# Second output layer of a fused attention and two-layer expert kernel: seven products in place of eight in five of six groups

## The chip, the cores and the metric

One core of a Trainium2 chip runs the whole program in one launch. The metric is the device time of that core in microseconds. Its engines are TensorE (PE; PEld is its weight load), VectorE (DVE), ScalarE (ACT), GpSimd (POOL) and the queue of SyncE (SP), which issues all DMAs here.

## The reference

```python
# q, k, v: (8, 8, 576, 64); x: 4608 tokens of 512 features; all float32
kv = einsum('bhsd,bhse->bhde', k, v)
out = einsum('bhsd,bhde->bhse', q, kv)
x = out / sqrt(mean(out * out, -1) + 1e-6) * g_norm     # -> (4608, 512)
x = (sigmoid(x @ w_gate) * (x @ w_val)) @ moe_w_out     # inner width 1536
h = x @ moe2_w_in                                       # inner width 2048
return where(h > 0, h, exp(min(h, 0)) - 1) @ moe2_w_out
```

All inputs and the output are float32. (Weights come as 64-bit words of which the kernel takes the upper and the lower 32 bits apart and puts a float32 together.)

## The kernel before

**Numbers.** A matmul operand is kept as two rounded parts, hi (ACT rounds, `x_hi`) and lo (DVE subtracts, `x_lo`); a product of two operands is three matmuls, hi·hi, hi·lo and lo·hi (`matmul3`, lines 347 to 351). So nearly all matmuls stand on lines 349 to 351.

**Groups.** The 4608 tokens are cut into 12 blocks of `BLK` = 384, two blocks to a group, `NG` = 6 groups. Features are cut into 128-row chunks. In the first half of the kernel (to about 985 us in the trace) each group has its attention (`attention`, for two blocks each), the first gated layer (`in1`, twelve products of 42 matmuls, and `in1_plain` for group 0) and the first output layer (`out1`), whose result goes to memory (`x2d`). The second half runs, group by group, `in2` and `out2`: eight pairs of hidden chunks in `in2`, and an output layer over `NF2` = 16 hidden chunks.

**Seven products.** The in layers already run as Strassen (Winograd) products in 2 x 2 blocks: the two token blocks of a group against the two halves of the features, and two chunks of hidden units. `quad` (line 484) takes seven products, six matmuls of 384 columns each, puts them into four PSUM banks `psi` and adds them with `plus` on DVE (line 500) into `v` tiles. `sides` (line 466) makes their left sides: differences of the token blocks, `k1` on DVE, `k2`, `k3` and the last one on POOL (lines 473 to 478), and hi and lo of seven sides (lines 479 and 480). `sums` makes the weights' sums on POOL and stores them in memory; `stream` loads hi and lo of them again for each group, 1 MB a tile of class `S` (five slots).

**The second output layer.** `out2` (line 619) is a plain product. For each of 16 hidden chunks and both token blocks, `split` (line 564) rounds a hidden tile of 128 x 384 into a `J` tile (ACT line 567, DVE line 569; three slots), and three token tiles of 128 are the stationary operand against 512 columns of weights: nine matmuls of 512 columns for each split, 288 a group, in six PSUM tiles. `copy_out` (lines 572 to 575) brings these to `kv` tiles, and six stores of 256 KB go to `out`.

**The norm.** In `attention` 13 small operations on DVE (lines 423 to 430) make the inverse root, written as one task (line 432), so that nothing else can come between them; four scalings (line 440) and the transposes (line 450) follow.

**Order.** `Plan` orders all tasks ahead of time, before the program runs: TensorE's tasks keep the order in which they are written, and each other engine takes, whenever it is idle in the plan, the ready task with the earliest due time. Each task has a planned duration, an engine, and the tiles that it holds; a class of tiles has a fixed number of slots and in places a cap by kind. On the chip each engine then runs its tasks in the planned order and waits by semaphore. `decode` (line 259) takes the weights apart during the first half; that of the second output layer stores hi and lo for a pair of chunks in `wo2`.

Of the kernel before, what the change touches and what calls it, by code (L numbers as in the profile page):

```python
# [21 lines left out]
P = 128  # L22
# [12 lines left out]
MM = BLK / 2400 + 0.0126  # L35
MMW = DM / 2400 + 0.0126
T_ACT, T_DVE, T_POOL = 0.53, 0.57, 1.15

# [167 lines left out]
def tile_kernel(ctx: ExitStack, tc: tile.TileContext, kv, kvtail, qt, g2, w1, w2, out):  # L206
# [30 lines left out]
    slots("psi", 4, [P, 512], F32, ps)  # L237
    slots("psa", 4, [P, 512], F32, ps)
    plan.caps.update({"h": 32, "tmp": 11, "xf": 8, "ev": 3, "q": 4, "dec": 4, "dec2": 2, "wh": 2, "wp": 2})
# [19 lines left out]
    def decode(layer, fp, after=None):  # L259
# [20 lines left out]
        sa = plan.buf("S", "dec" if layer in "gvo" else "dec2")  # L280
        if layer in "oO":
# [8 lines left out]
        if layer in "oO":  # L290
            d = (wo1 if layer == "o" else wo2)[fp]
            written[layer, fp] = [dma(P * 8192, lambda: nc.sync.dma_start(
                out=d.rearrange("q f t n -> q (f t n)"), in_=sa.slot.rearrange("q b t n -> q (b t n)").bitcast(F32)), [h, l], [sa])]
            return sa, [h, l]
        d = (ws2 if layer == "I" else ws1["gv".index(layer)])[fp]
# [8 lines left out]
    def sums(layer, fp, wh, w):  # L304


        d = (ws2 if layer == "I" else ws1["gv".index(layer)])[fp]
        sf, sb_ = plan.buf("wk", "wp"), plan.buf("S", "dec2" if layer == "I" else "st")
        A = lambda i: wh.slot[:, i // 2, i % 2 * 256:i % 2 * 256 + 256]
# [12 lines left out]
        return sb_, [h2, l2], st  # L322

    def fresh(layer, fp):

        sa, wh = plan.buf("S", "st"), plan.buf("wk", "wh")
        k = "gv".index(layer)
        ld = dma(P * 4096, lambda: nc.sync.dma_start(out=wh.slot, in_=wf1[k][fp]), written["f", layer, fp], [wh], early=20.0)
        ld_a = dma(P * 6144, lambda: nc.sync.dma_start(out=sa.slot[:, 1:4].bitcast(F32), in_=ws1[k][fp][:, 0:3]), written[layer, fp], [sa], early=15.0)
        sb_, done, st = sums(layer, fp, wh, ld)  # L330
        written[layer, fp] = written[layer, fp] + [st]
        return (sa, sb_), ([ld_a], done)

    def stream(layer, fp):

        sa = plan.buf("S", "st")
        if layer in "oO":
            d = (wo1 if layer == "o" else wo2)[fp]
            return sa, [dma(P * 8192, lambda: nc.sync.dma_start(
                out=sa.slot.rearrange("q b t n -> q (b t n)").bitcast(F32), in_=d.rearrange("q f t n -> q (f t n)")), written[layer, fp], [sa], early=15.0)]  # L340
        d = (ws2 if layer == "I" else ws1["gv".index(layer)])[fp]
        sb_ = plan.buf("S", "st")
# [39 lines left out]
    def attention(j, queue, direct=None, bank="psa", gap=3, hold=None):  # L382
# [82 lines left out]

    def sides(xa, xb):

        X = {c: plan.buf(c) for c in XB}
        done = {c: [] for c in XB}
        for c in range(2):  # L470
            (b11, d11), (b21, d21), (b12, d12), (b22, d22) = xa[c], xa[c + 2], xb[c], xb[c + 2]
            t1, t2 = plan.buf("v", "tmp"), plan.buf("v", "tmp")
            k1 = add("DVE", 0.5, lambda t=t1, a=b12, b=b11: nc.vector.tensor_tensor(t.slot, a.slot, b.slot, op=ALU.subtract), [d12, d11], [t1, b12, b11])  # L473
            k3 = add("POOL", T_POOL, lambda a=b22, b=b12: nc.gpsimd.tensor_tensor(b.slot, a.slot, b.slot, op=ALU.subtract), [k1, d22], [b22, b12])
            k2 = add("POOL", T_POOL, lambda t=t2, a=b22, b=t1: nc.gpsimd.tensor_tensor(t.slot, a.slot, b.slot, op=ALU.subtract), [k1, d22], [t2, b22, t1])  # L475
            for n, f, d in (("x11", b11, d11), ("xt2", t2, k2), ("x12", t1, k1), ("xt3", b12, k3), ("x21", b21, d21), ("x22", b22, d22), ("xt4", None, None)):
# [141 lines left out]

    def out2(g, hs):
        acc = {blk: [plan.buf("psi" if blk == 0 else "psa") for _ in range(TPB)] for blk in range(2)}  # L620
        for f in range(NF2):
            if f % 2 == 0:
                s, ld = stream("O", f // 2)
            for blk in in_blocks(f, NF2):
                j, dj = split(*hs[f // 2][f % 2, blk])
                for i in range(TPB):
                    def mm(i=i, blk=blk, j=j, s=s, f=f):
                        v = s.slot.rearrange("q b t n -> q (b t n)").rearrange("q (f t n) -> q f t n", f=2, t=2)
                        matmul3(acc[blk][i].slot, j.slot[:, 0, i * P:i * P + P], j.slot[:, 1, i * P:i * P + P],
                                v[:, f % 2, 0, :], v[:, f % 2, 1, :], f == 0, f == NF2 - 1)  # L630
                    t = add("PE", 3 * MMW, mm, ld + dj, [acc[blk][i], s, j])
                    if f == NF2 - 1:
                        e = plan.buf("kv")
                        view = lambda e=e: e.slot.rearrange("q a c n -> q (a c n)")[:, :DM]
                        c = copy_out(i, view, lambda b=acc[blk][i]: b.slot, [t], [e, acc[blk][i]])
                        r0 = (2 * g + blk) * BLK + i * P
                        dma(P * 2048, lambda view=view, r0=r0: nc.sync.dma_start(out=out[r0:r0 + P, :], in_=view()), [c], [e], due=0.5)


# [111 lines left out]
```

## Time and profile before

| | us |
|---|---|
| median of three runs | 1728.72 (1728.35 to 1732.57) |
| profiled execution | 1734.85 |
| its span, first to last instruction | 1733.0 |
| TensorE busy | 1699.8 |
| VectorE busy | 969.7 |
| ScalarE busy | 745.6 |
| GpSimd busy | 258.0 |

The profiled execution is one run, some microseconds longer than the median. Busy times are taken from the records of instructions: a matmul's record also covers the time in which its last columns pass through the array beside the next one's first, so the time that one takes is read from the distance of starts. The granted clock is TensorE's share of its 2.4 GHz level; it was 0.987 on average. A wait is told with the engine that waited, the line, and what released it.

### The profile page before, as it was taken

The numbers are of one execution on the slowest core, as the hardware profiler recorded it, in microseconds if no ns is written. First come the engines' busy times: TensorE is split into PE (matmuls) and PEld (weight loads), VectorE is DVE, ScalarE is ACT, GpSimd is POOL, SyncE is SP. The second block draws the span as 40 slices with busy tenths as digits, with TensorE's granted clock in tenths as the row PEclk, the third lists the DMA queues.
The fourth block names the chain that finished last, engine by engine and source line by source line (L and its number), as shares of the span: only waits on it lengthen the run. The fifth ranks groups of instructions, "written<-read, shape, count | busy, mean of one in ns | idle before, by whom it ended". The sixth has DMA issues, their size and how long they took to land.

```text
span 1733.0 us, 26330 instructions
## 1 busy us (share of the span) xinstructions
PE 1699.8 (98%) x9999; PEld 1596.4 (92%) x9999; DVE 969.7 (56%) x1752; ACT 745.6 (43%) x1495; POOL 258.0 (15%) x242
## 2 busy tenths in 40 slices
PE   8999999999999999999999999999999999999998
PEld 6899999989999999899899998898998998998987
DVE  5768466834585475458445465365465455555542
ACT  4556433632362254126213364364453453543542
POOL 0001264401231141124022001001001001001000
PEclk7999999999999999999999999999999999999999
DMA  8997987888579679767877465575574673673751
GB/s 311 336 310 267 347 274 286 307 311 302 217 291 344 228 257 344 273 219 266 316 256 261 166 259 196 185 265 182 192 273 150 220 280 119 249 272 110 265 200 58
DMA packets 94447, 431.65 MB, mean 249 GB/s; under 512 B 10608, under 2 KB 29040, under 8 KB 66928
## 3 DMA queue, kind: packets, MB, share of 16 engines
q1 hardware_dynamic: 94320, 429.96, 68.3%
q8 instruction: 79, 1.29, 0.3%
q14 instruction: 48, 0.39, 0.1%
HBM read 353.37 MB, written 76.55 MB: 248 GB/s over the span
## 4 chain that ended last, share of the span: by engine, by line
PE 91%; DMA 4%; DVE 3%; issue 1%; ACT 1%; SPq 0%; DVEq 0%; ACTq 0%
PE psi L349 23%; PE psi L351 22%; PE psi L350 22%; PE psa L350 7%; PE psa L351 6%; PE psa L349 6%; PE psa L407 2%; DMA S<-wsv 1%; PE psa L375 1%; DVE xp L440 1%; PE psa L450 1%; DMA wsI<-S 1%; DVE v L500 1%; DMA wsv<-S 1%; DMA wsg<-S 0%
## 5 line engine op out<-in xcount | busy, mean ns | idle before, releaser
L500 DVE TENSOR_TENSOR v<-v,psi 128x384 f32<-128x384 f32 x540 | 298.2, 553 | 355.8 <-PE psi L351 347.3
L349 PE MATMUL psi<-x,S 128*128 128x384 f32 x1056 | 361.3, 342 | 4.7 <-DVE v L500 4.0
L351 PE MATMUL psi<-x,S 128*128 128x384 f32 x1056 | 355.7, 337 | 4.8 <-DVE S L289 4.8
L350 PE MATMUL psi<-x,S 128*128 128x384 f32 x1056 | 355.1, 336 | 0.9 <-DVE x L458 0.9
L569 DVE TENSOR_TENSOR J<-v,J 128x384 fp32r<-128x384 f32 x336 | 201.8, 604 | 254.5 <-ACT J L567 254.3
L567 ACT ACTIVATE J<-v 128x384 fp32r<-128x384 f32 x336 | 175.3, 523 | 324.0 <-PE psa L350 116.7
L349 PE MATMUL psi<-xt,S 128*128 128x384 f32 x648 | 222.1, 343 | 11.2 <-DMA S<-wsv 7.4
L351 PE MATMUL psi<-xt,S 128*128 128x384 f32 x648 | 218.3, 337 | 0.0
L350 PE MATMUL psi<-xt,S 128*128 128x384 f32 x648 | 218.0, 336 | 0.0
L349 PEld LDWEIGHTS psi<-x,S 128*128 128x128 f32 x1056 | 199.7, 189 | 9.7 <-DVE v L500 5.9
L351 PEld LDWEIGHTS psi<-x,S 128*128 128x128 f32 x1056 | 199.7, 189 | 5.4 <-DVE S L289 5.4
L350 PEld LDWEIGHTS psi<-x,S 128*128 128x128 f32 x1056 | 199.8, 189 | 1.9 <-DVE x L458 1.4
L536 POOL TENSOR_TENSOR v<-v,v 128x384 f32<-128x384 f32 x90 | 97.0, 1083 | 419.4 <-DVE v L500 418.7
L475 POOL TENSOR_TENSOR v<-v,v 128x384 f32<-128x384 f32 x22 | 23.7, 1077 | 759.8 <-DVE v L473 580.0
L349 PEld LDWEIGHTS psi<-xt,S 128*128 128x128 f32 x648 | 122.8, 190 | 14.4 <-issue 8.1
L350 PEld LDWEIGHTS psi<-xt,S 128*128 128x128 f32 x648 | 122.9, 190 | 0.0
L351 PEld LDWEIGHTS psi<-xt,S 128*128 128x128 f32 x648 | 122.7, 189 | 0.0
L613 ACT ACTIVATE v<-v 128x384 f32<-128x384 f32 x144 | 75.4, 524 | 108.6 <-DVE v L500 108.6
L351 PE MATMUL psa<-S,J 128*128 128x512 f32 x288 | 112.8, 392 | 0.0
L351 PE MATMUL psi<-S,J 128*128 128x512 f32 x288 | 112.6, 391 | 0.0
L350 PE MATMUL psa<-S,J 128*128 128x512 f32 x288 | 112.2, 390 | 0.0
L349 PE MATMUL psi<-S,J 128*128 128x512 f32 x288 | 112.1, 389 | 0.0
(99 smaller groups left out, 2863.9 us busy)
## 6 DMA issues: line engine op xcount, KB each, us to landing
S<-wsI SPq DMA_DIRECT2D x48, 1024.0 KB, 5.1
S<-wsO SPq DMA_DIRECT2D x48, 1024.0 KB, 4.9
S<-wso SPq DMA_DIRECT2D x36, 1024.0 KB, 6.3
S<-wsI SPq DMA_DIRECT2D x48, 768.0 KB, 5.9
raw<-w SPq DMA_DIRECT2D x68, 512.0 KB, 6.4
S<-wsg SPq DMA_DIRECT2D x24, 1024.0 KB, 5.4
S<-wsv SPq DMA_DIRECT2D x24, 1024.0 KB, 5.1
S<-wsg SPq DMA_DIRECT2D x30, 768.0 KB, 6.6
```

What stands on the lines that cost most here:

```text
L349: nc.tensor.matmul(acc, wh, xh, start=first, stop=False, skip_group_check=more)
L350: nc.tensor.matmul(acc, wh, xl, start=False, stop=False, skip_group_check=more)
L351: nc.tensor.matmul(acc, wl, xh, start=False, stop=last, skip_group_check=more)
L375: nc.tensor.matmul(pb.slot[e, :D], k[:, 0, c, e], k[:, 1, c, e], start=(c == 0), stop=False)
L407: nc.tensor.matmul(o[h].slot[lo - t0:hi - t0, n:n + D], qs[k].slot[r, lo - j * BLK:hi - j * BLK], kvb[b % 2][r, 2 * pp + k, :], start=True ...
L440: norm[pp, h] = add("DVE", T_DVE, lambda x=xn[pp], o=po[pp][h], pp=pp, h=h: nc.vector.tensor_tensor(x.slot.rearrange("q k (i n) -> q (k i) ...
L475: k2 = add("POOL", T_POOL, lambda t=t2, a=b22, b=t1: nc.gpsimd.tensor_tensor(t.slot, a.slot, b.slot, op=ALU.subtract), [k1, d22], [t2, b22 ...
L500: return add("DVE", T_DVE, lambda: nc.vector.tensor_tensor(dst.slot, a.slot, bank[k].slot[:, :BLK], op=ALU.add), after, [dst, a, bank[k]])
L536: t = add("POOL", T_POOL, lambda r=r, b=b: nc.gpsimd.tensor_tensor(r.slot, r.slot, b.slot, op=ALU.mult), [d, s], [r, b])
L567: hi = add("ACT", T_ACT, lambda: nc.scalar.activation(j.slot[:, 0, :], f.slot, AF.Copy), [d], [j, f])
L569: lo = add("DVE", 0.5, lambda: nc.vector.tensor_tensor(j.slot[:, 1, :], f.slot, j.slot[:, 0, :].bitcast(F32), op=ALU.subtract), [hi], [j, f])
L613: a1 = add("ACT", T_ACT, lambda e=e, b=b: nc.scalar.activation(e.slot, ps_or_v(b), AF.Relu, scale=-1.0), [d], [e, b])
```

## The change

- `out2` of groups 1 to 5 is written as seven products as `quad` is: the hidden tiles of the two token blocks (`B11`, `B12`, `B21`, `B22`) against weights in four parts (two halves of the hidden chunks, two halves of 256 columns). A product runs over eight weight pairs, three token tiles and three terms with 256 columns. `combine` makes T1 to T3 on POOL and T4 on DVE, in `w` tiles, which are halves of the tiles `raw`, `wk` and `kv` that are free by then, or in place; each side of a product is split anew (7 x 8 splits in place of 32). Each product has two PSUM tiles, and `copy` (ACT) and `plus` (DVE) of 512 and 256 columns bring it into `xp` tiles, of which there are four. Four stores of 384 KB go to `out`.
- Group 0 keeps the plain product (`out2_plain`), reading the weights in their new layout, and out of `xp` tiles. Beside it `sums_O` loads each weight pair, makes four sums on DVE, splits them and stores them to `wo2`, which has eight parts now. POOL's first `combine` waits for all tasks that use `raw`, `wk` or `kv`.
- `sides` takes the engine as an argument; for the second layer its three POOL steps go to DVE.
- The norm's 13 operations are 13 tasks, except in the two blocks that are written with `hold` (the first two).
- `v` has 48 slots in place of 50, `xp` 4 in place of 3.

```diff
-    slots("xp", 3, [P, 2, BLK], F32)
-    slots("v", 50, [P, BLK], F32)
+    slots("xp", 4, [P, 2, BLK], F32)
+    slots("v", 48, [P, BLK], F32)
...
-    wo2 = [dr.tile([P, 2, 2, DM], F32, tag=f"wsO{f}", name=f"wsO{f}") for f in range(NF2 // 2)]
+    wo2 = dr.tile([P, 8, NF2 // 2, 2, 256], F32, tag="wsO", name="wsO")
...
+    def sums_O(fp, after):
+
+        pair, w = [(plan.buf("kv"), "q a c n -> q (a c n)"), (plan.buf("raw"), "q n t -> q (n t)")], plan.buf("wk", "wh")
...
+        for i in range(2):
+            ld = dma(P * 4096, lambda i=i: nc.sync.dma_start(out=v[i](), in_=wo2[:, 2 * i:2 * i + 2, fp]), written["O", fp] + [after], [pair[i][0]])
+            word.append(add("DVE", 0.7, lambda i=i: nc.vector.tensor_tensor(
+                W()[:, 2 * i:2 * i + 2, :], v[i]()[:, :, 0, :], v[i]()[:, :, 1, :], op=ALU.add), [ld], [pair[i][0], w]))
+        last = word
+        for d, a, b, op in ((1, 0, 1, ALU.add), (0, 2, 0, ALU.subtract), (2, 1, 2, ALU.subtract), (3, 3, 2, ALU.subtract)):
+            last = [add("DVE", 0.4, lambda d=d, a=a, b=b, op=op: nc.vector.tensor_tensor(one(d), one(a), one(b), op=op), last, [w])]
+        st = []
+        for i, src in ((0, lambda: W()[:, 1:3, :]), (1, lambda: W()[:, 0:4:3, :])):
...
+            st.append(dma(P * 4096, lambda i=i: nc.sync.dma_start(out=wo2[:, 4 + 2 * i:6 + 2 * i, fp], in_=v[i]()), [h, l], [pair[i][0]]))
...
-        last = [add("DVE", 0.2 * len(ops), lambda: [op() for op in ops], red, [sm])]
+        last = red
+        for part in ([ops] if hold is not None else [[op] for op in ops]):
+            last = [add("DVE", 0.2 * len(part), lambda part=part: [op() for op in part], last, [sm])]
...
-    def sides(xa, xb):
+    def sides(xa, xb, eng="POOL"):
+        ge, gt = (nc.gpsimd, T_POOL) if eng == "POOL" else (nc.vector, T_DVE)
...
+        def combine(x, y, dst=None, eng="POOL"):
+            res = []
+            for i, ((a, da), (b, db)) in enumerate(zip(x, y)):
+                d = dst[i][0] if dst else plan.buf("w")
...
+        def product(k, piece, side, first, last, after=()):
+            for f in range(n):
+                if f % 4 == 0:
+                    s = plan.buf("S", "st")
+                    ld = dma(P * 8192, lambda s=s, f=f: nc.sync.dma_start(out=s.slot.bitcast(F32), in_=wo2[:, piece, f:f + 4]),
+                             sum((written["O", i] + written["s", i] for i in range(f, f + 4)), []), [s], early=15.0)
+                src, d = side[f]
+                j, dj = split(src, d)
...
+                        nc.tensor.matmul(acc, x[0], w[:, 0], start=st, stop=False, skip_group_check=True)
+                        nc.tensor.matmul(acc, x[0], w[:, 1], start=False, stop=False, skip_group_check=True)
+                        nc.tensor.matmul(acc, x[1], w[:, 0], start=False, stop=last and f == n - 1, skip_group_check=True)
...
+        T1 = combine(B12, B11)
+        T2 = combine(B22, T1)
+        T3 = combine(B22, B12, B12)
+        p1 = product("a", 2, B11, True, True)
+        s1 = copy(t1, "a", [p1])
+        p5 = product("c", 4, T1, True, True)
+        p6 = product("b", 5, T2, True, True)
+        u2 = plus(t2, t1, "b", s1 + [p6])
+        u4 = plus(t1, t2, "c", u2 + [p5])
+        T4 = combine(B21, T2, T2, "DVE")
+        p7 = product("d", 6, T3, True, True)
+        c22 = plus(t1, t1, "d", u4 + [p7])
+        store(t1, 0, 1, c22)
+        p2 = product("a", 3, B21, False, True, s1)
+        store(t0, 1, 0, copy(t0, "a", [p2]))
+        p3 = product("c", 7, B22, False, True, u4)
+        c12 = plus(t3, t2, "c", u2 + [p3])
+        store(t3, 1, 1, c12)
+        p4 = product("d", 1, T4, False, True, c22)
+        c21 = plus(t2, t2, "d", c12 + [p4])
+        store(t2, 0, 0, c21)
...
-        X, done = sides(load_x2(g, 0), load_x2(g, 1))
-        out2(g, [in2(fp, X, done) for fp in range(NF2 // 2)])
+        X, done = sides(load_x2(g, 0), load_x2(g, 1), "DVE")
+        n = len(plan.pe)
+        (out2 if g else out2_plain)(g, [in2(fp, X, done) for fp in range(NF2 // 2)])
+        if g == 0:
+            for fp in range(NF2 // 2):
+                sums_O(fp, plan.pe[n + (len(plan.pe) - n) * fp // 9])
+            gate = add("POOL", 0.05, lambda: None, [t for t in plan.tasks if any(b.cls in ("raw", "wk", "kv") for b in t.bufs)])
```

## Rows read from the trace of the kernel before

**Rows 1.** Page, part 1: busy us, share of the span, instructions; all engines.

```profile
PE 1699.8 (98%) x9999; PEld 1596.4 (92%) x9999; DVE 969.7 (56%) x1752; ACT 745.6 (43%) x1495; POOL 258.0 (15%) x242
```

**Rows 2.** Timeline, second output layer: start, us, engine line op out<-in [idle before <-releaser].

```profile
1173.30 0.53 ACT L567 ACTIVATE J<-v 128x384 fp32r<-128x384 f32 x1 [1.51 <-PE psa L350]
1173.33 0.39 PE L349 MATMUL psi<-S,J 128*128 128x512 f32 x1
...
1173.86 0.56 DVE L569 TENSOR_TENSOR J<-v,J 128x384 fp32r<-128x384 f32 x1 [1.48 <-ACT J L567]
...
1175.37 0.39 PE L349 MATMUL psa<-S,J 128*128 128x512 f32 x1
```

**Rows 3.** Windows (out2 group 0, in2 group 1): length, PE, PEld, DVE, ACT, POOL busy, clock, DMA, GB/s.

```profile
1043.00:1109.00 66.00, 66.00 (x292) 54.20 (x291) 30.74 (x52) 24.35 (x50) 7.35 (x6) 1.00 0.47 170
1109.00:1167.00 58.00, 58.00 (x337) 58.00 (x336) 35.41 (x72) 33.99 (x74) 0.00 (x0) 1.00 0.73 261
```

**Rows 4.** Waits of TensorE: engine line <- releaser: us in total, times, longest.

```profile
PE psi L349 <- DVE v L500: 7.7, 10, 1.0
PE psi L349 <- DMA S<-wsv: 7.6, 4, 2.6
```

**Rows 5.** Timeline of TensorE in the first output layer, 384 columns.

```profile
156.62 0.33 PE L349 MATMUL psa<-J,S 128*128 128x384 f32 x1
...
158.70 0.33 PE L349 MATMUL psi<-J,S 128*128 128x384 f32 x1
```

**Rows 6.** Timeline of weight loads: transposes at 57 us, after a wait at 1078 us.

```profile
57.55 0.97 PEld L450 LDWEIGHTS psa<-ident,xp 128*128 128x128 f32 x8
57.73 0.93 PE L450 MATMUL psa<-ident,xp 128*128 128x128 f32 x7
...
1078.43 0.19 PEld L351 LDWEIGHTS psi<-S,J 128*128 128x128 f32 x1 [0.31 <-DVE J L569]
...
1078.54 0.19 PEld L349 LDWEIGHTS psi<-S,J 128*128 128x128 f32 x1
```

**Rows 7.** Timeline of VectorE and GpSimd, sides of the next group, same stretch.

```profile
1077.98 1.27 POOL L478 TENSOR_TENSOR v<-v,v 128x384 f32<-128x384 f32 x1 [0.49 <-DVE xt L480]
...
1078.30 1.37 DVE L480 TENSOR_TENSOR xt<-v,xt 128x384 fp32r<-128x384 f32 x1
...
1079.59 0.55 DVE L480 TENSOR_TENSOR x<-v,x 128x384 fp32r<-128x384 f32 x1
...
1080.05 0.55 DVE L569 TENSOR_TENSOR J<-v,J 128x384 fp32r<-128x384 f32 x1
```

**Rows 8.** Groups by line and shape: count | busy us, mean ns | idle before, releasers.

```profile
L500 DVE TENSOR_TENSOR v<-v,psi 128x384 f32<-128x384 f32 x540 | 298.2, 553 | 355.8 <-PE psi L351 347.3 <-ACT J L567 5.5 <-ACT v L614 1.1
...
L478 POOL TENSOR_TENSOR v<-v,v 128x384 f32<-128x384 f32 x22 | 28.8, 1318 | 11.3 <-DVE xt L480 11.3
...
L475 POOL TENSOR_TENSOR v<-v,v 128x384 f32<-128x384 f32 x22 | 23.7, 1077 | 759.8 <-DVE v L473 580.0 <-DVE x L480 149.6 <-ACT v L454 23.9
...
L574 DVE COPY kv<-psi 128x512 f32<-128x512 f32 x6 | 4.2, 692 | 15.1 <-PE psi L351 15.1
```

**Rows 9.** Windows, GpSimd alone: busy, clock, DMA share, GB/s of the stage's first 6 us.

```profile
1043.00:1049.00 6.00, 0.00 (x0) 1.00 0.91 351
```

**Rows 10.** DMA issues: out<-in, count, KB each, median us to landing.

```profile
S<-wsO SPq DMA_DIRECT2D x48, 1024.0 KB, 4.9
```

**Rows 11.** Timeline of the end, ScalarE: the last two copies out of PSUM.

```profile
1728.73 1.26 ACT L575 ACTIVATE kv<-psa 128x512 f32<-128x512 f32 x2 [1.59 <-DVE kv L574]
```

**Rows 12.** Timeline of VectorE and TensorE around one norm chain.

```profile
237.97 0.17 DVE L423 TENSOR_SCALAR sm<-sm 128x24 f32<-128x24 f32 x1
...
240.92 1.95 DVE L440 TENSOR_TENSOR xp<-psa,sm 128x384 f32<-128x384 f32 x4
...
243.38 0.44 PE L349 MATMUL psi<-x,S 128*128 128x384 f32 x1 [0.90 <-DVE v L500]
```

More of the change, by code (lines that the diff above doesn't have):

```diff
@@ L36 @@
 MMW = DM / 2400 + 0.0126
+MMN = 256 / 2400 + 0.0133
 T_ACT, T_DVE, T_POOL = 0.53, 0.57, 1.15
@@ L238, in tile_kernel @@
     slots("psa", 4, [P, 512], F32, ps)
+    plan.slots["w"] = [t.bitcast(F32)[:, i * BLK:i * BLK + BLK] for t in
+                       [x.rearrange("q n t -> q (n t)") for x in plan.slots["raw"]] + [x.rearrange("q f n -> q (f n)") for x in plan.slots["wk"]]
+                       + [x.rearrange("q a c n -> q (a c n)") for x in plan.slots["kv"]] for i in range(2)]
     plan.caps.update({"h": 32, "tmp": 11, "xf": 8, "ev": 3, "q": 4, "dec": 4, "dec2": 2, "wh": 2, "wp": 2})
@@ L322, in sums @@
         return sb_, [h2, l2], st
+    def sums_O(fp, after):
+        pair, w = [(plan.buf("kv"), "q a c n -> q (a c n)"), (plan.buf("raw"), "q n t -> q (n t)")], plan.buf("wk", "wh")
+        v = [lambda b=b, o=o, n=n: b.slot.bitcast(F32).rearrange(o, **n)[:, :1024].rearrange("q (i t n) -> q i t n", i=2, t=2)
+             for (b, o), n in zip(pair, ({}, {}))]
+        W = lambda: w.slot.rearrange("q f (k n) -> q (f k) n", k=2)
+        one = lambda i: W()[:, i, :]
+        word = []
+        for i in range(2):
[7 more added lines that the diff above has]
+        for i, src in ((0, lambda: W()[:, 1:3, :]), (1, lambda: W()[:, 0:4:3, :])):
+            r = lambda i=i, t=0: v[i]()[:, :, t, :].bitcast(F32R)
+            h = add("ACT", 0.65, lambda r=r, src=src: nc.scalar.activation(r(), src(), AF.Copy), last, [pair[i][0], w])
+            l = add("DVE", 0.7, lambda r=r, src=src: nc.vector.tensor_tensor(r(t=1), src(), r().bitcast(F32), op=ALU.subtract), [h], [pair[i][0], w])
+            st.append(dma(P * 4096, lambda i=i: nc.sync.dma_start(out=wo2[:, 4 + 2 * i:6 + 2 * i, fp], in_=v[i]()), [h, l], [pair[i][0]]))
+        written["s", fp] = st
     def fresh(layer, fp):
@@ L336, in stream @@
         sa = plan.buf("S", "st")
-        if layer in "oO":
-            d = (wo1 if layer == "o" else wo2)[fp]
+        if layer == "o":
+            d = wo1[fp]
             return sa, [dma(P * 8192, lambda: nc.sync.dma_start(
                 out=sa.slot.rearrange("q b t n -> q (b t n)").bitcast(F32), in_=d.rearrange("q f t n -> q (f t n)")), written[layer, fp], [sa], early=15.0)]
+        if layer == "O":
+            return sa, [dma(P * 8192, lambda: nc.sync.dma_start(out=sa.slot.bitcast(F32), in_=wo2[:, 0:4, fp]), written[layer, fp], [sa], early=15.0)]
         d = (ws2 if layer == "I" else ws1["gv".index(layer)])[fp]
@@ L637, in out2, with mm, copy, plus @@
                         dma(P * 2048, lambda view=view, r0=r0: nc.sync.dma_start(out=out[r0:r0 + P, :], in_=view()), [c], [e], due=0.5)
+    def out2(g, hs):
+        n = NF2 // 2
+        bank = {k: (plan.buf("psi"), plan.buf("psa")) for k in "abcd"}
+        blk = {k: [hs[f][k] for f in range(n)] for k in ((0, 0), (0, 1), (1, 0), (1, 1))}
+        def combine(x, y, dst=None, eng="POOL"):
+            res = []
+            for i, ((a, da), (b, db)) in enumerate(zip(x, y)):
+                d = dst[i][0] if dst else plan.buf("w")
+                e, t = (nc.gpsimd, T_POOL) if eng == "POOL" else (nc.vector, T_DVE)
+                t = add(eng, t, lambda e=e, d=d, a=a, b=b: e.tensor_tensor(d.slot, a.slot, b.slot, op=ALU.subtract),
+                        [da, db] + used.get(d, []) + ([] if dst else [gate]), [d, a, b])
+                for x in {a, b} - {d}:
+                    used.setdefault(x, []).append(t)
+                res.append((d, t))
+            return res
+        used = {}
+        def product(k, piece, side, first, last, after=()):
[6 more added lines that the diff above has]
+                j, dj = split(src, d)
+                used.setdefault(src, []).extend(dj)
+                def mm(s=s, j=j, f=f):
+                    w = s.slot[:, f % 4]
+                    for i in range(TPB):
+                        acc = bank[k][i // 2].slot[:, i % 2 * 256:i % 2 * 256 + 256]
+                        x = [j.slot[:, t, i * P:i * P + P] for t in range(2)]
+                        st = first and f == 0 and i % 2 == 0
+                        nc.tensor.matmul(acc, x[0], w[:, 0], start=st, stop=False, skip_group_check=True)
+                        nc.tensor.matmul(acc, x[0], w[:, 1], start=False, stop=False, skip_group_check=True)
+                        nc.tensor.matmul(acc, x[1], w[:, 0], start=False, stop=last and f == n - 1, skip_group_check=True)
+                m = add("PE", 9 * MMN, mm, [ld] + dj + list(after), [bank[k][0], bank[k][1], s, j])
+            return m
+        B11, B12, B21, B22 = blk[0, 0], blk[0, 1], blk[1, 0], blk[1, 1]
+        wide = ((0, lambda t: t.slot.rearrange("q a n -> q (a n)")[:, :512], 512, 0.7), (1, lambda t: t.slot.rearrange("q a n -> q (a n)")[:, 512:], 256, 0.43))
+        def copy(dst, k, after):
+            return [add("ACT", t, lambda i=i, v=v, w=w: nc.scalar.activation(v(dst), bank[k][i].slot[:, :w], AF.Copy), after, [dst, bank[k][i]])
+                    for i, v, w, t in wide]
+        def plus(dst, a, k, after):
+            return [add("DVE", t, lambda i=i, v=v, w=w: nc.vector.tensor_tensor(v(dst), v(a), bank[k][i].slot[:, :w], op=ALU.add), [x for x in after if x is not None], [dst, a, bank[k][i]])
+                    for i, v, w, t in wide]
+        def store(t, half, b, after):
+            r0 = (2 * g + b) * BLK
+            dma(P * 3072, lambda: nc.sync.dma_start(
+                out=out[r0:r0 + BLK, half * 256:half * 256 + 256].rearrange("(i p) c -> p i c", p=P),
+                in_=t.slot.rearrange("q a n -> q (a n)").rearrange("q (i c) -> q i c", c=256)), after, [t], due=0.5)
+        t1, t2, t3, t0 = (plan.buf("xp") for _ in range(4))
+        T1 = combine(B12, B11)
[19 more added lines that the diff above has]
+        store(t2, 0, 0, c21)
```

34 lines of the change are left out of this document (20 added, 14 removed).

## The prediction

> **What bounds the kernel now.** I read the page first: TensorE is busy 98% of the span and every other engine 56% or less [rows 1]. A busy TensorE says little, because recorded matmuls overlap, so I went on to start-to-start times. In the second output layer one matmul of 512 columns follows the other every 0.2267 us (nine from 1173.33 to 1175.37) [rows 2], and a group's stage holds 16 x 2 x 3 x 3 = 288 of them: 288 x 0.2267 = 65.3 us. The windows view shows that these stages have no gap: 66.00 us busy of 66.00, and the in-layer stages 58.00 of 58.00, at a granted clock of 1.00 of the 2.4 GHz level [rows 3]. DVE is busy 30.7 us and ACT 24.3 us of an output stage, so neither is the bound there. From 985 us on, only fewer or shorter matmuls shorten the kernel. Ahead of 985 us TensorE does wait; the waits view of TensorE lists it: 7.7 us in ten waits for DVE's sums out of PSUM (line 500) and 7.6 us in four for weights from memory [rows 4].
>
> **The output layer: matmuls.** In groups 1 to 5 a product has 8 weight pairs x 3 token tiles x 3 terms = 72 matmuls of 256 columns, and there are seven: 504 in place of 288 of 512. Columns fall from 147,456 to 129,024, to 7/8, but each matmul has a cost that its width doesn't pay. No row of before shows one of 256 columns from rounded inputs, so I bound it. With 384 columns the starts are 0.1733 us apart (twelve in 2.08 us) [rows 5]; against 0.2267 us for 512 that is 0.0534 us for 128 columns, and the straight line gives 0.1733 - 0.0534 = 0.1199 us for 256. The floor that could break the line is the weight load, one for each matmul. Recorded, a load takes 0.19 us, which would be an upper end of 0.19 us, a loss: 504 x 0.19 = 95.8 us a stage. But loads overlap: after a short wait two start 0.11 us apart (1078.43 and 1078.54), and the seven 128-column transposes at 57.73, each with its own load, take 0.93 us together, at most 0.13 each [rows 6]. A load every 0.11 us fits under a matmul of 0.12. The lower end is the columns alone, 0.0534 x 2 = 0.107 us, but the 512 and 384 rows both carry the same fixed 0.013, so I take 0.1199 us: 504 x 0.1199 = 60.4 us. That is 4.86 us less a stage, 24.3 us for five. Break-even is at 65.3 / 504 = 0.1296 us.
>
> **What feeds them.** Each block of nine matmuls needs a new J tile: ACT rounds, DVE takes the rest (lo). A block lasted 2.04 us and lasts 1.08 now, and splits go from 32 to 56 a stage. In the rows, ACT starts at 1173.30 as the block ahead has gone into the array, and DVE ends at 1173.86 + 0.56 = 1174.42: 1.12 us from a slot's release to full [rows 2]. With three slots it is wanted again two blocks later, after 2.16 us, so about 1 us may be lost in queues. DVE's occupancy goes by starts, 0.46 us apart where it is dense (1079.59, 1080.05) [rows 7], and not by the 0.55 us recorded. A stage of groups 1 to 4 asks of DVE 56 splits and 8 sums for the last input (64 x 0.47 = 30.1 us), five pairs of PSUM sums of 512 and 256 columns (a 512-column copy is recorded with 0.692 us [rows 8], so by the ratio of starts some 0.62 + 0.31 us, 4.6 us in all), and the next group's sides, 8 differences and 14 rests (22 x 0.47 = 10.3 us): 45 us of 60.4. ACT: 70 roundings at about 0.43 and four copies, some 32 us. Both fit, but a queue at 75% is not empty: behind a split there may lie a side's operation (0.47) or a product's sums (0.93 to 1.9), which fit into the 1 us or not. Bounds: nothing, and 2 us a stage (one late split of 0.3 us behind each of seven products); I take 0.5 us, as such bursts come with seven products and a sorted queue puts the earlier need first: 2.5 us in all.
>
> **The sums on POOL.** T1, T2, T3 are 24 operations a stage, 1.08 us each in the row of line 475 and 1.32 in that of line 478, which runs beside DVE's rests [rows 8]: 26 to 32 us. Their inputs come out of the in-layer stage, one pair every 58 / 8 = 7.25 us, and 16 of the 20 lent slots (two in each of ten tiles) are enough, so 21 of 24 can run while POOL is idle in that stage (no instruction in its 58 us [rows 3]). Beside POOL a DVE operation with two SBUF inputs takes 1.37 us in place of 0.55 (1078.30 beside POOL's 1077.98, against 0.55 at 1079.59), and the rest for a J tile that came late behind that made TensorE's weight load at 1078.43 wait 0.31 us [rows 6, 7]. DVE's sums out of PSUM are not hurt: 553 ns on average over all 540 [rows 8], with POOL beside many of them. So in the in-layer only the four last steps of the ELU and the sides can be slowed by some 0.8 us, under the two products (2.08 us) that lie between such a sum and its use; I price it at nothing, and at 1 us a stage if that cover fails. The sides' three POOL steps a half go to DVE in all six groups (36 x 0.47 = 17 us in sum), which takes away the collisions just shown and costs TensorE nothing, as DVE has 30 us free.
>
> The Trainium skill (SBUF — State Buffer, "SBUF: two separate sides") calls the port that DVE and GpSimd share an exclusive lock, which an operation with two SBUF inputs and a GpSimd operation take in turn for whole instructions. The trace agrees: 1.37 us against 0.55. Were the sums on POOL to run beside the splits, this rule would speak against the change; that is the rival C below.
>
> **The rest.** Group 0 keeps its plain products and gets the weights' sums: eight times, on DVE, four operations of 512 columns and four of 256, 4 x 0.62 + 4 x 0.31 = 3.7 us, 30 us over some 123 us of two stages in which DVE is busy 35.4 + 30.7 us [rows 3]: covered; 0 to 2 us, I take 0.5. Its 16.8 MB of traffic come on top of 261 GB/s in the in-layer, where the link has shown 351 [rows 3, 9], so half will slip into the plain products (170 GB/s), and nothing waits for it before group 1's second product. In groups 1 to 5 a stage now loads 14 x 1.05 MB and moves 3.1 MB of input and output: 17.8 MB in 60.4 us, 295 GB/s, below 351. A weight tile lasts 4.3 us and lands in 4.9 [rows 10], with five slots: hidden; without cover, 0.6 us a tile. The last stores wait for two sums (0.93 us) where two copies of 1.26 us stood [rows 11]: nothing. The stage holds all eight PSUM banks in turn; its first product needs one of the four that the in-layer uses, and the second product of the last seven has freed one by then: nothing, and a sum's 0.55 us a stage if not. On SP an output store or a store of `sums_O` waits for DVE with weight loads queued behind it, which five slots of 4.3 us each keep 17 us ahead; on DVE a product's sum waits for TensorE with the next lo behind it, which is the 0.5 us above; on POOL the first `combine` waits for group 0's tasks with only other sums behind it.
>
> The **norm** chain is one block on DVE: it starts at 237.97, 13 steps of some 0.2 us, and then four scalings (240.92, 1.95 us) go ahead of the sum that the next product waits for, with 0.90 us of wait at 243.38 [rows 12]. Cut into 13 pieces it lets sums of line 500 in between. Of the 7.7 us [rows 4] the scalings' burst can keep half, so I take 4 us; bounds are 8 us and a loss of 4, because with two v slots fewer, one xp slot more and another planned order the waits for loads (7.6 us) may fall otherwise.
>
> **Sum.** -24.3 + 2.5 + 0.5 - 4 = -25.3 us. The profiled execution took 1734.85 us, 1733.0 of it span, and would come to 1709.5; it was 6.1 us above the median of the runs, which I take over as it is: 1728.7 - 25.3 = 1703.4 us.
>
> **The rivals.** *B, the feed gives part of it back.* For it: three J slots, 1 us of room, DVE at 75%, and the 0.31 us wait [rows 6]. Against: stages with 32 splits show no gap. 1.5 to 3 us a stage: 7.5 to 15 us where I have 2.5, so 1708 to 1716, and with a norm that brings nothing up to 1720.
> *C, slower: POOL's sums collide with the splits.* Place: POOL runs T1 to T3 during the products, for want of slots or by order. Each of 24 then holds one DVE operation for 0.82 us more: 45 + 24 x 0.82 = 64.7 us of DVE, which is where the stage was, and a feed at that load adds one late split in three (19 x 0.3 = 5.7 us): 70 us, 1728.7 + 5 x 5 - 4 = 1750. It decides from about 20 collisions. Against: inputs are there a stage earlier and POOL is idle.
> *D, slower: the weight load bounds.* At 0.19 us: 5 x 30.5 us more, 1877 us; at 0.13 us only the norm's 4 us are left, 1725. Against: rows 6.
> *E, the change doesn't do what it says: fewer columns, but the link bounds.* 17.8 MB at the in-layer's 261 GB/s would be 68 us: 1738; at 351, 51 us, hidden. Against: that stage isn't bound by its link either.
>
> **How the numbers follow.** Forecast (1694 to 1708) 0.60, B 0.26, C 0.05, D 0.04, E 0.05. The likeliest is 1703.4. The range reaches from no late split and all the norm's waits gone (1728.7 - 24.3 - 8 = 1696, less 2 for the order) to B with no gain from the norm: 1694 to 1719. Measurement can tell some 0.3%, 5 us, from no change: faster than 1723.5 is 0.60 + 0.26 + 0.01 of E; same 0.02 of D and 0.03 of E, 0.05; slower the rest, 0.05 + 0.02 + 0.01 = 0.08.
>
> **What would show it.** Starts of the 256-column matmuls 0.120 us apart; stages of 60.5 to 61.5 us; TensorE's waits for J below 3 us in all; POOL's sums ahead of each stage; fewer waits for line 500. Wrong, if these starts are over 0.125 us apart, or if DVE's rests show 1.3 us inside the products.

## The result, and the profile after

| | us |
|---|---|
| before, median on the chip of the comparison | 1730.58 |
| changed, median of four runs | 1703.99 (1701.89 to 1706.29) |
| ratio | 0.9847, 95% interval 0.9826 to 0.9868 |
| changed, profiled execution and its span | 1706.29, 1704.5 |

The forecast was 1703.4 us, and faster. The same kernel measured once more gave a ratio of 0.9831 (0.9808 to 0.9855), so the two measurements say, by their ratios, 26 and 29 us less.

The page of the changed kernel, part 1 (busy us, share, instructions), answers to [rows 1]:

```profile
PE 1672.8 (98%) x11079; PEld 1630.3 (96%) x11079; DVE 1127.8 (66%) x2052; ACT 809.6 (47%) x1631; POOL 346.3 (20%) x326
```

TensorE is as full as it was, with 1,080 more matmuls in a span that is 28.5 us shorter; VectorE went from 56% to 66%, GpSimd from 15% to 20%.

The windows view of group 1 (in-layer, then output stage) and of group 2's in-layer, with the columns of [rows 3] (the numbers in brackets count instructions):

```profile
1102.60:1161.30 58.70, 58.60 (x337) 58.18 (x336) 40.86 (x76) 34.43 (x75) 23.19 (x21) 1.00 0.83 305
1161.30:1222.40 61.10, 60.67 (x505) 60.47 (x505) 50.24 (x97) 36.86 (x75) 3.53 (x3) 1.00 0.86 294
1222.40:1280.60 58.20, 58.20 (x338) 58.20 (x337) 41.60 (x73) 32.64 (x72) 23.40 (x21) 1.00 0.70 252
```

Here the plan of the sums on GpSimd is to be read off the counts: 21 of them in the in-layer and three in the output stage. VectorE is busy 50.2 us of 61.1 by its records, and TensorE 60.67 of 61.10: 0.43 us of a stage is a wait.

The timeline of TensorE at the stage's first and last matmuls, and ten in its middle:

```profile
1161.31 0.28 PE L714 MATMUL psi<-S,J 128*128 128x256 f32 x1
```

```profile
1199.76 0.28 PE L714 MATMUL psi<-S,J 128*128 128x256 f32 x1
...
1200.84 0.28 PE L714 MATMUL psi<-S,J 128*128 128x256 f32 x1
```

```profile
1222.44 0.34 PE L384 MATMUL psi<-x,S 128*128 128x384 f32 x1
```

Nine starts lie between 1199.76 and 1200.84: 0.120 us for a matmul of 256 columns. The stage runs from 1161.31 to 1222.44, 61.13 us; the next three take 61.13 to 61.15, and the last takes 61.01 from its first start to its last, to which one matmul of 0.12 comes. 504 x 0.120 = 60.5, so 0.6 us of a stage is lost. Where it goes stands in the timeline, 2 to 6 us after the stage's start:

```profile
1162.96 1.03 POOL L689 TENSOR_TENSOR kv<-v,v 128x384 f32<-128x384 f32 x1 [3.21 <-DVE v L653]
1163.01 2.69 DVE L607 TENSOR_TENSOR J<-v,J 128x384 fp32r<-128x384 f32 x2
...
1164.07 1.22 POOL L689 TENSOR_TENSOR kv<-v,kv 128x384 f32<-128x384 f32 x1
...
1165.25 1.33 POOL L689 TENSOR_TENSOR v<-v,v 128x384 f32<-128x384 f32 x1
...
1165.62 1.37 DVE L653 SCALAR_TENSOR_TENSOR v<-v,v 128x384 f32<-128x384 f32 x1
...
1166.91 1.48 DVE L607 TENSOR_TENSOR J<-v,J 128x384 fp32r<-128x384 f32 x3
1167.51 0.19 PEld L716 LDWEIGHTS psi<-S,J 128*128 128x128 f32 x1 [0.63 <-DVE J L607]
1167.52 0.39 PE L716 MATMUL psi<-S,J 128*128 128x256 f32 x1 [0.43 <-DVE J L607]
```

GpSimd makes T1, T2 and T3 of the last pair, for which it had waited until VectorE's ELU step (line 653) gave it the input. Beside them VectorE needs 2.69 us for two lo's of J tiles and 1.37 us for its last ELU step, where one such step takes 0.55 alone. The next lo comes behind these, and the weight load of that lo waits 0.63 us. It is one wait in each of the five stages, always at this place, as the waits view of TensorE says (us in total, times, longest), here with the lines that answer to [rows 4]:

```profile
PE psi L384 <- DMA S<-wsv: 10.8, 6, 2.9
...
PE psi L384 <- DVE v L538: 2.2, 2, 2.0
PE psi L716 <- DVE J L607: 2.1, 5, 0.4
```

The waits for sums out of PSUM (line 500, now 538) fell from 7.7 us in ten to 2.2 us in two; those for weights from memory grew from 7.6 to 10.8. The profile of the second measurement tells which of the two belongs to the kernel:

```profile
PE psi L384 <- DMA S<-wsv: 5.2, 4, 2.7
...
PE psi L384 <- DVE v L538: 2.4, 3, 2.0
```

The waits for sums are there again, and those for weights differ from one execution to the next. In the profiled executions the first half ends at 979.1 us in place of 985.0 (and at 967.3 in the second measurement), and the second half takes 725.4 in place of 748.0 (725.7 in the second measurement).

### The profile page after: what moved, and what is told of

It reads as the page before. It is cut to its first block, busy times and chain, and to the rows that moved or that the text cites. A ratio compares the mean times of both kernels' runs of the same rounds, so it can differ in the third digit from the quotient of the medians.

```text
span 1704.5 us, 29344 instructions
## 1 busy us (share of the span) xinstructions
PE 1672.8 (98%) x11079; PEld 1630.3 (96%) x11079; DVE 1127.8 (66%) x2052; ACT 809.6 (47%) x1631; POOL 346.3 (20%) x326
## 4 chain that ended last, share of the span: by engine, by line
PE 92%; DMA 3%; DVE 3%; issue 1%; ACT 0%; SPq 0%; DVEq 0%; ACTq 0%
PE psi L384 20%; PE psi L386 20%; PE psi L385 20%; PE psi L716 4%; PE psi L714 4%; PE psi L715 4%; PE psa L385 3%; PE psa L386 3%; PE psa L384 3%; PE psa L442 2%; DMA S<-wsv 2%; PE psa L716 2%; PE psa L714 2%; PE psa L715 2%; PE psa L410 1%; PE psa L487 1%
## 5 line engine op out<-in xcount | busy, mean ns | idle before, releaser
L574 POOL TENSOR_TENSOR v<-v,v 128x384 f32<-128x384 f32 x90 | 97.5, 1089 | 427.6 <-DVE v L538 368.5
L716 PE MATMUL psi<-S,J 128*128 128x256 f32 x560 | 159.0, 284 | 2.1 <-DVE J L607 2.1
L714 PE MATMUL psi<-S,J 128*128 128x256 f32 x560 | 158.4, 283 | 0.0
L715 PE MATMUL psi<-S,J 128*128 128x256 f32 x560 | 158.4, 283 | 0.0
L542 ACT ACTIVATE v<-psi 128x384 f32<-128x384 f32 x108 | 53.0, 491 | 145.6 <-PE psi L386 144.6
L716 PEld LDWEIGHTS psi<-S,J 128*128 128x128 f32 x560 | 107.4, 192 | 3.2 <-DVE J L607 3.2
```

Source lines behind the costliest of these rows:

```text
L542: s1 = add("ACT", T_ACT, lambda: nc.scalar.activation(t1.slot, bank["a"].slot[:, :BLK], AF.Copy), [p1], [t1, bank["a"]])
L574: t = add("POOL", T_POOL, lambda r=r, b=b: nc.gpsimd.tensor_tensor(r.slot, r.slot, b.slot, op=ALU.mult), [d, s], [r, b])
L714: nc.tensor.matmul(acc, x[0], w[:, 0], start=st, stop=False, skip_group_check=True)
L715: nc.tensor.matmul(acc, x[0], w[:, 1], start=False, stop=False, skip_group_check=True)
L716: nc.tensor.matmul(acc, x[1], w[:, 0], start=False, stop=last and f == n - 1, skip_group_check=True)
```

## The experiments

Each ratio is against the kernel before on the same chip.

### The parts alone

**The norm alone**, on the kernel before:

```diff
-        last = [add("DVE", 0.2 * len(ops), lambda: [op() for op in ops], red, [sm])]
+        last = red
+        for part in ([ops] if hold is not None else [[op] for op in ops]):
+            last = [add("DVE", 0.2 * len(part), lambda part=part: [op() for op in part], last, [sm])]
```

> The kernel before with the norm of ten blocks cut into 13 tasks each, and nothing else. Theory (the uncut norm held up the sums of line 500): TensorE's waits for line 500 fall from 7.7 us to under 4, the first half ends 3 to 6 us earlier, the kernel takes 1725 (ratio 0.997), with the second half as it was (748 us). Rival (the first half of the changed kernel ended 5.9 us earlier by its other slots or by chance of the order): no difference over 1 us.

Ratio 0.9956 (0.9943 to 0.9968): 7.6 us less than 1733.3, nearly twice what the prediction gave it. Its waits view:

```profile
PE psi L349 <- DMA S<-wsv: 5.8, 4, 2.2
...
PE psi L349 <- DVE v L502: 3.4, 2, 3.2
```

The mechanism is shown: waits for the sums (line 502 here) are down from 7.7 to 3.4 us and from ten to two, and the output stages keep their 65.7 us. That makes 4.3 of the 7.6 us. The waits for weights are 1.8 us less too, but they change as much between executions of one kernel, so the rest of the 7.6 is not traced to a wait.

**The seven products alone**: the changed kernel with each norm as one task.

```diff
-        for part in ([ops] if hold is not None else [[op] for op in ops]):
+        for part in [ops]:
```

> The changed kernel with every norm as one task again. Theory: the output stages keep their 61.1 us and give 5 x 4.6 = 23 us, the first half is as before to 2 us (985 us): 1708 (ratio 0.987). Rival (the norm has no part in it): the first half ends at 979 as in the changed kernel, ratio 0.9847. Second rival (slots and order cost something that the norm hides): the first half ends after 987.

Ratio 0.9869 (0.9850 to 0.9888), 22.7 us. The waits view:

```profile
PE psi L384 <- DVE v L538: 8.1, 11, 1.2
PE psi L384 <- DMA S<-wsv: 6.5, 3, 2.6
...
PE psi L716 <- DVE J L607: 2.1, 5, 0.4
```

The output stages take 61.14 us as in the changed kernel, and the waits for the sums are back, 8.1 us in eleven. Its profiled execution ended its first half at 977.9 us all the same; that execution was the fastest of four (1705.3 to 1713.3), so how long the first half of one execution takes doesn't settle a matter of 5 us. The medians say 1709.5 us here, against 1708 expected.

**The slots alone**: `v` 48 and `xp` 4 in the kernel before.

```diff
-    slots("xp", 3, [P, 2, BLK], F32)
-    slots("v", 50, [P, BLK], F32)
+    slots("xp", 4, [P, 2, BLK], F32)
+    slots("v", 48, [P, BLK], F32)
```

> The kernel before with 48 v slots in place of 50 and four xp slots in place of three. Theory (the slots matter little; the norm alone gives the first half's gain): within 2 us of the kernel before. Rival (the norm cut alone gave 7.6 us and the seven products alone 22.7, which is 3.7 us more than both together; two v slots fewer take that back): 2 to 6 us more than the kernel before.

Ratio 0.9999 (0.9987 to 1.0010): nothing. Its waits view:

```profile
PE psi L349 <- DVE v L500: 7.7, 9, 1.3
```

The norm is uncut here and the waits for the sums are those of the kernel before, 7.7 us, yet the first half of this execution ended at 978.3 us in place of 985.0. So the end of the first half in a single profile can't show what the norm brings; the row of the waits and the medians can. The two other parts give 7.6 + 22.7 = 30.3 us, and the changed kernel 26 and 29 in its two measurements, which agrees within the intervals.

> The changed kernel once more, beside the others on the same chip. Theory: ratio 0.983 to 0.986. Rival (the first measurement was lucky or not): outside of that.

This is the second measurement named above: 0.9831 (0.9808 to 0.9855).

### The cost of a narrow matmul

Each matmul of the last group's output stage cut into two of 128 columns:

```diff
+                            for c in range(2 if g == NG - 1 else 1):
+                                k2 = slice(c * 128, c * 128 + 128) if g == NG - 1 else slice(0, 256)
+                                nc.tensor.matmul(acc[:, k2], x[y], w[:, u, k2], start=st and y == 0 and u == 0 and c == 0, stop=last and f == n - 1 and y == 1, skip_group_check=True)
```

> The changed kernel with each matmul of the last group's output stage as two of 128 columns, 1008 with a weight load each. Theory (a weight load can be had every 0.108 us and no faster, a matmul of 256 columns takes 0.107 us of columns and 0.013 us besides): starts 0.108 us apart, the stage takes 109 us in place of 61.0, the kernel 48 us more than the changed one. Rival (a fixed cost for each matmul and no floor): 0.053 + 0.013 = 0.067 us apart, 67 us, 6 us more. Second rival (a load costs its recorded 0.19 us somewhere): over 0.15 us apart.

The windows view of that last stage with the kernel's end (columns as above), and the weight loads in it by the timeline:

```profile
1634.50:1751.30 116.80, 112.72 (x1010) 112.57 (x1008) 42.64 (x76) 31.06 (x61) 3.48 (x3) 0.99 0.33 114
```

```profile
1659.89 0.75 PEld L717 LDWEIGHTS psa<-S,J 128*128 128x128 f32 x6
1660.56 0.42 PEld L717 LDWEIGHTS psi<-S,J 128*128 128x128 f32 x3
```

The kernel took 1753.1 us in its single execution, 49 us more than the changed kernel's median, where 48 were expected. The 1008 matmuls take 112.4 us from the first start to the last, 0.112 us each. The six loads from 1659.89 to the next at 1660.56 are 0.67 / 6 = 0.112 us apart. The straight line of the widths would have given 67 us. So the floor is there, a load and its matmul every 0.112 us, and 256 columns at 0.120 stand just above it: the recorded 0.19 us of a load is not its price, and a matmul of half the columns costs nearly as much as one of 256. The Trainium skill (TensorE: Matmul & The Clock Gate, "LDWEIGHTS (loading the stationary operand)") puts a load at its columns over 1.2 GHz, 0.107 us for 128; these runs come near it, with 0.112 us between loads.

Could the floor be a price of every matmul, whatever it loads? The attention of the kernel before, whose matmuls load 64 columns, says no:

```profile
121.71 0.69 PE L375 MATMUL psa<-kv 128*64 128x64 f32 x16
122.33 0.33 PE L377 MATMUL psa<-tail 64*64 64x64 f32 x4
```

Sixteen of them start within 0.62 us, 0.039 us apart. They are narrower in both operands, so they don't give the price of a smaller load.

### The feed and GpSimd

**The sides of the second layer on GpSimd again:**

```diff
-        X, done = sides(load_x2(g, 0), load_x2(g, 1), "DVE")
+        X, done = sides(load_x2(g, 0), load_x2(g, 1))
```

> The changed kernel with the second layer's sides on GpSimd again, six operations a stage. Theory (two-input steps of VectorE wait for GpSimd, about 0.8 us each): four to six splits or rests a stage are held up inside the products, stages of 61.7 to 63 us in place of 61.1, so 2 to 8 us more than the changed kernel. Rival (three J slots have 1 us of room, which hides a single hold-up of 0.8): stages of 61.1 to 61.3, less than 1 us more.

Ratio 0.9916 (0.9902 to 0.9930): some 12 to 15 us more than the changed kernel, where 2 to 8 were expected. Stages of groups 1 to 4 take 64.0 to 65.0 us, the last, which has no sides to make, 61.1. Together with 1.3 us more in group 0's stage these make 15.5 us. The windows view of group 2's stage and one place in it by the timeline:

```profile
1280.50:1345.40 64.90, 62.44 (x505) 60.82 (x504) 52.15 (x91) 36.60 (x75) 11.00 (x9) 1.00 0.81 277
```

```profile
1305.74 1.22 POOL L513 TENSOR_TENSOR v<-v,v 128x384 f32<-128x384 f32 x1 [20.01 <-DMA v<-x2d]
...
1305.99 1.38 DVE L689 TENSOR_TENSOR wk<-v,wk 128x384 f32<-128x384 f32 x1
...
1306.91 1.33 POOL L512 TENSOR_TENSOR v<-v,v 128x384 f32<-128x384 f32 x1
...
1307.29 1.37 DVE L607 TENSOR_TENSOR J<-v,J 128x384 fp32r<-128x384 f32 x1
...
1308.59 0.68 DVE L728 TENSOR_TENSOR xp<-xp,psi 128x512 f32<-128x512 f32 x1
1308.72 0.19 PEld L716 LDWEIGHTS psi<-S,J 128*128 128x128 f32 x1 [0.40 <-DVE J L607]
...
1309.18 0.41 DVE L728 TENSOR_TENSOR xp<-xp,psa 128x256 f32<-128x256 f32 x1
...
1310.11 0.19 PEld L716 LDWEIGHTS psi<-S,J 128*128 128x128 f32 x1 [0.26 <-DVE J L607]
```

Two of GpSimd's steps follow each other, and hold two of VectorE's. The room of a split is gone with that, and behind them stand a product's sums (line 728, 512 and 256 columns), so that the next lo is late too, at 1310.11. The longest wait of this stage, 0.95 us at 1315.96, comes in the same way behind GpSimd's next two steps. Single hold-ups of 0.8 us would, by the prediction's sum, have fitted into the room of 1 us; they don't come singly. Six steps cost 3 to 4 us a stage.

**GpSimd's sums late**: in the plan all 24 wait for the last product of the in-layer.

```diff
+        in_last = plan.pe[-1]
...
-                        [da, db] + used.get(d, []) + ([] if dst else [gate]), [d, a, b])
+                        [da, db] + used.get(d, []) + ([] if dst else [gate]) + ([in_last] if eng == "POOL" else []), [d, a, b])
```

> The changed kernel with GpSimd's 24 sums of a group made to wait for the last product of the in-layer, so that they run beside the splits. Theory (the rival C of the prediction): each of 24 holds one two-input step of VectorE, VectorE is full and the stage takes 66 to 75 us in place of 61.1, so 25 to 70 us more than the changed kernel: slower than the kernel before. With GpSimd's six side steps the stage grew by 3.7 us, 0.6 us a step, which would make 24 x 0.6 = 15 us, 76 us a stage. Rival (the room of 1 us a split hides single hold-ups): stages under 63 us.

Ratio 0.9969 (0.9953 to 0.9985): 20 us and more of the gain are gone, though the kernel isn't slower than before, against the expectation; the norm's gain is still in it. Stages take 65.5 to 67.1 us. Group 2's in-layer, its output stage and 3.4 us of that by the windows view, and a stretch of the stage by the timeline:

```profile
1224.70:1282.90 58.20, 58.20 (x338) 58.20 (x337) 36.35 (x73) 33.12 (x72) 7.14 (x7) 1.00 0.70 252
1282.90:1349.90 67.00, 64.95 (x506) 62.64 (x505) 59.99 (x97) 37.04 (x75) 21.99 (x17) 0.97 0.79 268
...
1307.90:1311.30 3.40, 3.40 (x18) 3.40 (x17) 3.29 (x7) 0.85 (x2) 0.00 (x0) 0.50 0.11 42
```

```profile
1292.47 3.90 POOL L689 TENSOR_TENSOR wk<-v,raw 128x384 f32<-128x384 f32 x3
...
1292.84 3.94 DVE L607 TENSOR_TENSOR J<-kv,J 128x384 fp32r<-128x384 f32 x3
1292.97 0.19 PEld L717 LDWEIGHTS psi<-S,J 128*128 128x128 f32 x1 [0.16 <-DVE J L607]
...
1294.26 0.19 PEld L717 LDWEIGHTS psi<-S,J 128*128 128x128 f32 x1 [0.16 <-DVE J L607]
...
1295.55 0.19 PEld L717 LDWEIGHTS psi<-S,J 128*128 128x128 f32 x1 [0.16 <-DVE J L607]
```

While GpSimd works, one of its sums and one lo take turns, and a block is 1.29 us (1292.97, 1294.26, 1295.55) in place of 1.08. That is the mechanism of rival C.

But the run isn't rival C in full: GpSimd made seven sums in the in-layer and 17 in the output stage, and not 24. The added wait orders the plan alone, and no tile ties the sums of the first seven pairs to the last product. On the chip T1 of these pairs ran as soon as its inputs were there, and the other sums stand behind the eighth T1 in GpSimd's order. And the granted clock fell to 0.50, the 1.2 GHz level, for some 3 us in the stages of groups 2 and 4, shortly after waits of 1.2 and 0.4 us; group 3 had the same two waits and kept its clock. The three stages with a clock of 1.00 throughout take 65.5 to 65.9 us. So 17 sums beside the splits cost 4.4 to 4.8 us a stage, and 24 were not measured; in proportion they would cost some 6 to 7 us, an estimate.

**Two J slots in place of three:**

```diff
-    slots("J", 3, [P, 2, BLK], F32R)
+    slots("J", 2, [P, 2, BLK], F32R)
```

> The changed kernel with two J slots in place of three. Theory (a slot takes 1.12 us from release to full, and with two it is wanted again after one block of 1.08 us): each of 56 blocks waits some 0.1 to 0.3 us, stages of 67 to 78 us in the five groups, 30 to 85 us more than the changed kernel; the layers with blocks of 2 us stay within 1 us a stage. Rival (lo is wanted by the third matmul of a block alone, and two slots are enough): stages under 63 us.

Ratio 1.0023 (1.0010 to 1.0036): slower than before by 4 us, than the changed kernel by some 31 to 33. The windows view of group 2's stage and the waits view:

```profile
1292.40:1358.30 65.90, 64.49 (x505) 61.77 (x505) 50.99 (x98) 37.08 (x76) 3.51 (x3) 1.00 0.80 273
```

```profile
PE psa L385 <- DVE J L607: 9.2, 7, 1.6
PE psi L716 <- DVE J L607: 5.3, 11, 0.6
```

A stage takes 64.3 to 66.5 us, less than the 67 that I expected at least: five stages lose 3.3 to 5.4 us each, 23 in all. The rest is in the first output layer, which I took for safe: its products (line 385) now wait 9.2 us in seven waits for J. So the third slot carries most of the gain: without its 1.08 us of room the products wait.

### Without the one wait that is left

**The last pair's three sums on VectorE**, and **all sums on VectorE**:

```diff
+                on = "DVE" if i == n - 1 else eng
-                e, t = (nc.gpsimd, T_POOL) if eng == "POOL" else (nc.vector, T_DVE)
+                e, t = (nc.gpsimd, T_POOL) if on == "POOL" else (nc.vector, T_DVE)
```

```diff
-        def combine(x, y, dst=None, eng="POOL"):
+        def combine(x, y, dst=None, eng="DVE"):
```

> The changed kernel with T1, T2 and T3 of the last pair of a group on VectorE in place of GpSimd, three of 24. Theory: the one wait that each stage has, 0.59 us some 6 us after its start, comes from these three beside the first splits; it goes, stages last 60.5 us, 2.9 us less than the changed kernel in all. Rival (that wait comes from the last ELU steps that lie before the splits on VectorE): the wait stays, or grows by the added operations; 0 to 2 us more.

> The changed kernel with T1, T2 and T3 all on VectorE, GpSimd out of the second layer. Theory: VectorE has the time (41 us of 58 busy in the in-layer, some of it held up by GpSimd, and 24 x 0.47 = 11 us added), the wait of 0.59 us a stage goes, 60.5 us a stage: 2 to 3 us less than the changed kernel. Rival (more on VectorE delays the sums of the in-layer's products): in-layers longer than 58.3 us by 0.5 us or more each, no gain or a loss.

Ratios 0.9823 (0.9809 to 0.9837) and 0.9807 (0.9784 to 0.9830). The windows views of group 1, the first kernel's output stage, and the second's in-layer and output stage:

```profile
1158.80:1219.20 60.40, 60.40 (x505) 60.40 (x504) 49.52 (x100) 36.80 (x75) 0.00 (x0) 1.00 0.87 297
```

```profile
1102.70:1161.00 58.30, 58.30 (x337) 58.26 (x337) 44.34 (x91) 34.25 (x74) 0.00 (x0) 1.00 0.83 298
1161.00:1221.50 60.50, 60.50 (x507) 60.50 (x506) 51.86 (x106) 36.96 (x76) 0.00 (x0) 1.00 0.87 296
```

TensorE is busy throughout, and the stages take 60.3 to 60.5 us in both, which is 504 x 0.120. So the wait of 0.6 us came from GpSimd's three sums, and VectorE has the time for all 24: 44.3 us of 58.3 in the in-layer, hardly more than the 40.9 with GpSimd's help, since what GpSimd took off it came back as held-up steps. With all sums on VectorE the ratio is the lowest of all kernels here (median 1698.2 us). Against the changed kernel the intervals overlap (0.9807 against 0.9847 and 0.9831), so the total doesn't show a gain; by the stages it is 0.67 us x 5 = 3.4 us.

Group 1's in-layer is 0.4 us shorter here too (58.3 against 58.7), but GpSimd's sums have no part in that. In the changed kernel the wait stands at 1108.12, and GpSimd's first sum starts at 1127.82:

```profile
1105.65 0.69 DVE L612 COPY xp<-psa 128x512 f32<-128x512 f32 x1 [2.53 <-DMA out<-xp]
...
1108.12 0.19 PEld L384 LDWEIGHTS psi<-x,S 128*128 128x128 f32 x1 [0.42 <-DVE v L538]
```

VectorE's last copy of group 0's output waits 2.53 us for a store to free its `xp` tile, and one of the rests of the weights' sums and then the in-layer's sums come behind it. In the profile with all sums on VectorE that wait is 1.74 us, and TensorE loses nothing.

## Why the prediction was right

- **The matmul of 256 columns**: 0.1199 us by the line through 384 and 512 columns [rows 2, 5], measured 0.120. Two widths always give a straight line, so its reach down to 256 was a guess until measured; that loads don't bound it was argued from [rows 6] and is shown by the narrow matmuls, at 0.112 us. Four of the five stages fell from 65.7 us (start to start, with waits of 0.4 us behind GpSimd's sides) to 61.1, and the last, which has no sides beside it, from 65.3 to 61.1: 22.5 us in all, where the sum had 24.3 - 2.5 = 21.8. The 0.4 us a stage was missing in the prediction: it took the stages of before as free of waits by [rows 3], whose busy time covers a wait as short as that at 1078.43 [rows 6]. Group 0's plain stage, with its neighbour's sides on VectorE, now takes 65.3.
- **The feed**: 0.5 us a stage by choice between 0 and 2, measured 0.6. The size was right and the cause another: not the product's sums in front of a lo, as I had it, but GpSimd's last three sums, which the prediction counted (21 of 24 fit into the in-layer) and didn't price. Without them nothing is lost, as the two kernels with VectorE's sums show. One of the prediction's own signs of being wrong, rests of 1.3 us inside the products, did appear: two in each stage (2.69 us at 1163.01). The sign was drawn too sharply, as two such rests cost 0.6 us a stage and no more.
- **GpSimd's sums in the in-layer**: priced at nothing, and so it was: in-layers take 58.25 us in groups 2 to 5 as before, though VectorE's records there grew from 35.4 us [rows 3] to 41.6.
- **The sides on VectorE**: "takes away the collisions and costs TensorE nothing" held, but the prediction gave it no size. With the seven products it is worth 3 to 4 us a stage; without this part half of the gain would be gone.
- **Group 0's sums**: 0.5 us put in. The in-layer beside them is 58.2 us as before, and the plain stage takes 65.3 in place of 65.7, which is the sides' doing. Group 1's in-layer takes 58.7 in place of 58.3, by the wait for a store told above with one of these rests behind it: 0.4 us. The size was right; that the copies of group 0's output would wait for stores stands nowhere in the prediction.
- **The norm**: 4 us taken between a loss of 4 and 8, measured alone 7.6 (5.5 to 9.9 by the interval). I let the four scalings keep half of the waits; with the chain cut, waits for the sums fell from 7.7 us to 3.4 alone and to 2.2 and 2.4 in the changed kernel, so 4.3 to 5.5 us are traced to the mechanism, and the term was somewhat too small. The loss that I feared from the slots measured nothing.
- **Rivals**: C's mechanism is real. Its price is tested for 17 sums and not for 24: the rival put the break-even at about 20 collisions, and with 17 the stage is where it was before (65.5 to 65.9 us). By the estimate above 24 would give some 67 to 68 us in place of its 70. D and E are out: loads every 0.112 us, and the link carried 294 GB/s (295 expected).

By the halves of the profiled executions, the second is 22.6 us shorter (21.3 in the sum) and the first 5.9 (4). Only the second is evidence: the first half of one kernel ended at 979.1 and at 967.3 us in two profiles. The five stages' 22.5 us and the 5.3 to 5.5 us of waits for sums come to some 28 us, in line with the 26 and 29 measured. That the total came within 1 us of the median is luck: the two measurements of the ratio alone differ by 2.8 us.

## What to carry to other kernels

Ask of each cut in matmul columns at what width the weight load takes over: here the 1/8 fewer columns of a Winograd product brought 7.4% of the stage, and half the width would have brought a loss. Shorter blocks use up the feed's slack before they use up its engines: count, in time and not in busy share, what may stand in front of a split, and keep GpSimd's two-input work out of that stretch or give it to VectorE altogether. A long chain of tiny operations planned as one task holds up whatever the full engine waits for behind it; such chains cost TensorE 7.7 us of waits here, and cutting them was worth a third of the seven products. A wait that only orders a plan doesn't hold an engine on the chip: 7 of 24 sums ran early in spite of one.

## What the runs showed of the hardware

- In a run of 1008 matmuls, weight loads of 128 x 128 for rounded float32 operands followed each other every 0.112 us, though each is recorded with 0.19 us; matmuls of 128, 256, 384 and 512 columns with such loads start 0.112, 0.120, 0.173 and 0.227 us apart.
- VectorE's step with two inputs in SBUF and GpSimd's take turns when both are queued: 1.29 us for a pair (one sum of 384 columns and one lo), against 0.46 us from start to start for VectorE's steps alone [rows 7].
- The stores of the output landed after 5.4 us (median) in the changed kernel, 384 KB in rows of 1 KB and group 0's 256 KB in rows of 2 KB alike, where the 256 KB stores took 2.1 before. So the length of the rows is not shown to be the cause; the queue carried more (a mean of 282 GB/s in place of 249), and which of its loads matters stays open. One of group 0's stores held VectorE up for 2.53 us.
